# Gate sums begun one unit of four slots later, and eleven weight casts moved one quarter slot earlier, in a gated attention and feed-forward kernel

## The chip, the core and the metric

The kernel runs on one core of a Trainium2 chip. The metric is device time in microseconds (us) of one launch, the median of several runs. Engines are named as in the profile: PE (TensorE matmuls) and PEld (its weight loads), DVE (VectorE), ACT (ScalarE), POOL (GpSimd), and SP, whose queue issues most of the DMAs. A line "L230" is line 230 of the kernel before.

## The reference

```python
x = A_x                                   # 1 x 2048 x 512, float32
g = sigmoid((x * gate_w).sum(-1, keepdims=True))
# attention: 32 heads of 16, causal window of 256 keys
q, k, v = split(x @ wqkv)
o = softmax(mask(q @ k.T * 16 ** -0.5)) @ v
a = o @ wo
# feed-forward, 1792 hidden
b = (silu(x @ w_gate) * (x @ w_up)) @ w_down
return g * a + (1 - g) * b
```

Everything is float32 in and out. The row sum under the sigmoid is what the kernel calls the gate sum: one product and sum over 512 columns for each of 2048 rows, so 16 blocks of 128 rows.

## The kernel before, in words

**Precision.** A float32 matmul is done as three matmuls on halves: each operand is split into a high half (a cast to fp32r, `wh` for a weight, on ACT at L67) and a low half (operand minus high half, `wl`, on POOL at L70), and high x high, high x low and low x high are summed in PSUM. So every weight block of 128 x 512 comes in by DMA as `raw` (L75, one buffer), is cast by ACT and subtracted by POOL before PE can use it. The next `raw` can only be fetched when POOL has read the last one.

**Stages.** A first stage (to about 93 us) makes the projections of the first two groups of heads and V. The second stage, up to about 605 us, is attention, with the feed-forward's gate and up projections and the later groups' q and k projections mixed in. The third stage does the down projection and the output projection.

**Slots, quarters, units.** The attention stage is an order written out by hand: 128 slots t = 0 to 127 (8 groups of 4 heads x 16 blocks of 128 rows), each of four quarters hd = 0 to 3. In each quarter PE gets one score matmul of the next group for the row maximum (`stage1`, L280; DVE adds the mask and takes the maximum, L282), one score matmul of the present group (`stage2`, L319; ACT takes the exponential, L321, POOL masks it, L323 and L326) and six matmuls of a projection (L230). PSUM for each of the two score matmuls has two buffers, so the L319 of a quarter needs the exponential of two quarters before, and L280 needs the maximum of two quarters before. From slot 112 on there is no `stage1`. Four slots are a unit (`unit`): two pairs of projections, into the PSUM tiles `pa` in the unit's slots 0 and 2 and `pb` in its slots 1 and 3. In the first slot of each unit, after quarter 1, come the probability x V matmuls of the last unit (`av`, L343), and `finish` (L358 to L373) normalises them in five steps, the first an ACT copy, the second a DVE addition (L360) that frees `pb`.

I write (t, hd) for a quarter. Everything else is hung on quarters by `later(t, hd, f)`: what is registered for a quarter is emitted after that quarter's matmuls, in the order of registration. For a unit of feed-forward gates two tanh (L531) are emitted at its (2, 3) and (3, 0), that is in the unit's slot 2, quarter 3, and slot 3, quarter 0, and their products (L534) at (3, 0) and (3, 1).

**Weights.** For each weight block the loop over `KEYS` (L517 to L522) hangs two things on quarters: the split (ACT cast and POOL subtraction) and the DMA that fetches the next block. `t` is the slot in which the weight is first used. If the buffers come free only in the last slot before t, the split stands at (t - 1, 1) and the fetch at (t - 1, 3). Thirteen of the blocks are of this kind, first used at slots 8, 20, 32, 40, 52, 64, 72, 84, 96, 104, 112, 120 and 128.

**Gate sums.** `gate_place` (L591) fetches gate_w into a tile that the q and k halves have left free, `gate_fetch` (L595) fetches a block of x, two buffers in turn, `gate_block` (L598) multiplies and sums it on DVE (L599). Block b's fetch is hung behind the sum of block b - 2. `gate_end` (L606) turns the 16 sums into the sigmoid (an exponential on ACT, L607, and three short DVE operations, L608 to L610). Between slots 96 and 112 two blocks are summed in a unit, after that three. g7 in the code is 112.

**Row maxima.** Every eighth slot `put_max` (L293, L294) negates and transposes the maxima on DVE and sends them through DRAM (L296, L298); it is emitted at quarter 2 of a unit's first slot, just ahead of the addition L360.

Of the kernel before, what the change touches and what calls it, by code (L numbers as in the profile page):

```python
# [19 lines left out]
NB = S // P  # L20
# [13 lines left out]
def gated_mix(ctx, tc, xT, xn, wqk, wv, wo, wgu, wd, gw, out):  # L34
# [70 lines left out]
    def halves_of(t):  # L105
        n = t.shape[-1] // 2
        return [t[:, :n], t[:, n:]]
# [49 lines left out]
    PEND = []  # L157
# [21 lines left out]
    with ExitStack() as A:  # L179
# [312 lines left out]
        for n, turn in enumerate(turns):  # L492
            for m, _ in enumerate(turn, 3 * NK * n):
                at = [max(0, i - wait) * 2 * NB // (total - wait) for i in (m, m + 1)]
# [19 lines left out]
        def later(t, hd, *fs):  # L514
            AT.setdefault((t, hd), []).extend(fs)

        for n, key in enumerate(KEYS[:-1]):  # L517
            if n:
                t, free = FIRST[key], LAST.get(KEYS[n - 2], 0) + 1 if n > 1 else 0
                at = (t - 1, int(n > 1)) if t % 4 else (t - 2, 0) if free < t - 1 else (t - 1, 1)  # L520
                later(*at, lambda: PEND.pop(0)())
                later(*((t, 0) if t % 4 else (at[0], at[1] + 2)), prefetch)  # L522

        SIL = {}

# [61 lines left out]
        g7 = (G - 1) * NB  # L587
# [7 lines left out]
        def gate_fetch(b):  # L595
            nc.sync.dma_start(XG[2 + b % 2], xn[b * P:(b + 1) * P])

        def gate_block(b):  # L598
            nc.vector.scalar_tensor_tensor(XG[1], XG[2 + b % 2], 1.0, XG[0], op0=ALU.mult, op1=ALU.mult,  # L599
                                           accum_out=gate[:, b:b + 1])  # L600
# [9 lines left out]
            nc.vector.tensor_scalar(igate, gate, -1.0, 1.0, op0=ALU.mult, op1=ALU.add)  # L610

        pieces = [h for two in (QT[0], KT[0], QT[1], KT[1]) for t in two for h in halves_of(t)]
        blocks = [(t, n) for t in range(g7 - 12, g7 + NB, 4) for n in (range(1, 3) if t < g7 else range(3))][:NB]
        blocks = [(t + n, 3 - (n > 0)) for t, n in blocks]
        later(g7 - 13, 1, gate_place)
        for b in range(NB):
            t, hd = blocks[b]
            later(t, hd, lambda b=b: gate_block(b))
            if b > 1:
                t, hd = blocks[b - 2]  # L620
                later(t + hd // 3, (hd + 1) % 4, lambda b=b: gate_fetch(b))
            else:
                later(g7 - 13 + b, 2, lambda b=b: gate_fetch(b))
        later(g7 + NB - 3, 2, gate_end)
        for m in range(NB // 2):
            wd_early(m)

# [235 lines left out]
```

## Time and profile before

| | |
|---|---|
| three runs, us | 828.31, 828.32, 831.07 (median 828.32) |
| the profiled execution, us | 830.57, of which the span of instructions is 828.9 |
| PE busy, share of the span | 99% |
| PEld, DVE, ACT, POOL busy | 84%, 64%, 48%, 42% |
| mean granted TensorE clock | 0.998 |
| DMA traffic | 105.98 MB, mean 128 GB/s |

The profile gives for each instruction its start and duration in us from the span's start, its line, what it writes and reads, and, where its engine stood idle ahead of it, for how long and which other instruction or DMA ended that. Matmuls overlap, so a PE that is "busy" 99% can still lose time: what counts is the distance between the starts of matmuls. A quarter slot is measured from the first L280 or L319 of it to the first of the next.

### The profile page before, as it was taken

What the parts mean: (1) busy time and instruction counts of PE and PEld (TensorE: products, weight loads), DVE (VectorE), ACT (ScalarE), POOL (GpSimd) and SP (SyncE); (2) the same over time, 40 slices, a digit from 0 to 9 for tenths busy, and PEclk for the clock granted to TensorE, in tenths of its full rate; (3) what the DMA queues carried; (4) which work ended last, traced back from release to release, by engine and by line L of the source; (5) the groups of instructions that cost most, each with busy time, mean ns of one, the idle gap of its engine ahead of it and who ended that gap; (6) DMA issues with size and microseconds to landing.
All of it is one profiled execution on the core that took longest, in us unless ns stands there. A gap on an engine that the chain in (4) does not pass through costs nothing.

```text
span 828.9 us, 21356 instructions
## 1 busy us (share of the span) xinstructions
PE 821.0 (99%) x8329; PEld 694.9 (84%) x8329; DVE 530.7 (64%) x1494; ACT 401.0 (48%) x831; POOL 349.4 (42%) x639
## 2 busy tenths in 40 slices
PE   9999999999999999999999998999999999999998
PEld 7888998888889879888888887887888888888886
DVE  6396787778777777887787787876664332321322
ACT  6423556566556665566566554555532322222231
POOL 7712455465546564545556544465511211011020
PEclk9999999999999999999999999999999999999999
DMA  8584414514333435152453352453476331241501
GB/s 292 162 226 134 141 66 133 160 49 151 107 107 118 121 131 148 39 173 75 112 163 110 98 163 100 135 188 124 142 245 203 106 126 59 99 144 53 157 8 51
DMA packets 52980, 105.98 MB, mean 128 GB/s; under 512 B 9936, under 2 KB 14672, under 8 KB 52880
## 3 DMA queue, kind: packets, MB, share of 16 engines
q1 hardware_dynamic: 48912, 90.73, 35.8%
q0 software_dynamic: 3968, 13.90, 4.6%
q8 instruction: 65, 1.06, 0.6%
q14 instruction: 35, 0.29, 0.1%
HBM read 47.45 MB, written 31.98 MB: 96 GB/s over the span
## 4 chain that ended last, share of the span: by engine, by line
PE 96%; DMA 1%; DVE 1%; SPq 0%; POOL 0%; issue 0%; ACT 0%; DVEq 0%
PE pb L230 24%; PE pa L230 23%; PE pb L343 7%; PE ps L86 6%; PE ps L85 6%; PE ps L87 6%; PE ps L280 6%; PE ps L319 5%; PE pb L210 2%; PE ps L343 2%; PE pb L86 2%; PE pb L85 2%; PE pb L87 2%; PE pa L745 1%; PE pb L745 1%; PE pa L210 1%
## 5 line engine op out<-in xcount | busy, mean ns | idle before, releaser
L282 DVE CUSTOM_DVE_ANT_0 ps<-ps,mask 128x384 f32<-128x384 f32 (+2 forms) x512 | 269.3, 540 | 109.0 <-PE ps L280 51.3
L321 ACT ACTIVATE pt<-ps 128x384 f32<-128x384 f32 (+2 forms) x512 | 239.4, 475 | 134.9 <-PE ps L280 70.2
L323 POOL TENSOR_SCALAR_AFFINE_SELECT pt<-pt 128x256 f32<-128x256 f32 x256 | 109.4, 427 | 221.9 <-ACT pt L321 220.4
L280 PE MATMUL ps<-k,q 63*128 63x384 f32 (+2 forms) x512 | 159.7, 332 | 2.0 <-DVE mx L282 2.0
L319 PE MATMUL ps<-q,k 64*128 64x384 f32 (+2 forms) x512 | 160.5, 332 | 0.1
L230 PE MATMUL pb<-xhi,wh 64*128 64x512 f32 x512 | 115.2, 395 | 0.4 <-DVE o L360 0.4
L230 PE MATMUL pb<-xlo,wh 64*128 64x512 f32 x512 | 113.6, 391 | 0.0
L230 PE MATMUL pb<-xhi,wl 64*128 64x512 f32 x512 | 113.5, 392 | 0.0
L230 PE MATMUL pa<-xhi,wh 64*128 64x512 f32 x512 | 113.2, 395 | 0.0
L230 PE MATMUL pa<-xhi,wl 64*128 64x512 f32 x512 | 112.4, 396 | 0.0
L230 PE MATMUL pa<-xlo,wh 64*128 64x512 f32 x512 | 112.0, 393 | 0.0
L70 DVE TENSOR_TENSOR hl<-got,hh 128x512 fp32r<-128x512 f32 x51 | 44.3, 870 | 97.8 <-ACT hh L67 97.8
L280 PEld LDWEIGHTS ps<-k,q 63*128 63x128 f32 x512 | 89.0, 185 | 19.1 <-issue 5.7
L326 POOL TENSOR_SCALAR_AFFINE_SELECT pt<-pt 128x256 f32<-128x256 f32 x224 | 96.0, 429 | 0.0
L319 PEld LDWEIGHTS ps<-q,k 64*128 64x128 f32 x512 | 90.8, 185 | 4.9 <-issue 0.8
L343 PE MATMUL ps<-pt,vg 64*32 64x320 f32 (+4 forms) x1408 | 75.0, 346 | 0.0
L343 PE MATMUL pb<-pt,vg 64*32 64x320 f32 (+3 forms) x1360 | 73.9, 350 | 0.0
L282 DVE DVE_READ_ACCUMULATOR2_ANT mx<- 128x1 f32 x512 | 71.7, 140 | 0.0
L343 PEld LDWEIGHTS pb<-pt,vg 64*32 64x32 f32 x1360 | 46.3, 106 | 28.1 <-DVE ev L546 6.2
L230 PEld LDWEIGHTS pb<-xhi,wh 64*128 64x128 f32 x512 | 60.5, 185 | 6.7 <-DVE o L360 1.1
L230 PEld LDWEIGHTS pa<-xhi,wl 64*128 64x128 f32 x512 | 58.4, 185 | 8.6 <-POOL wl L70 3.0
L230 PEld LDWEIGHTS pb<-xhi,wl 64*128 64x128 f32 x512 | 60.3, 184 | 5.0
(162 smaller groups left out, 1557.0 us busy)
## 6 DMA issues: line engine op xcount, KB each, us to landing
kept_h<-ev SPq DMA_DIRECT2D x52, 256.0 KB
got<-kept_h SPq DMA_DIRECT2D x51, 256.0 KB
od<-o POOLq DMA_DIRECT2D x32, 256.0 KB, 3.6
raw<-wgu SPq DMA_DIRECT2D x28, 256.0 KB
q<-xhi SPq DMA_DIRECT2D x56, 128.0 KB
k<-xhi SPq DMA_DIRECT2D x56, 128.0 KB
vd<-vs POOLq DMA_DIRECT2D x8, 672.0 KB, 4.8
vg<-vd SPq DMA_DIRECT2D x32, 168.0 KB
```

The source lines that it names most:

```text
L70: lo_eng.tensor_tensor(out=lo, in0=src, in1=hi.bitcast(F32), op=ALU.subtract)
L85: nc.tensor.matmul(ps, lh, rh, start=start and i == 0, stop=False, skip_group_check=skip)
L86: nc.tensor.matmul(ps, lh, rl, start=False, stop=False, skip_group_check=skip)
L87: nc.tensor.matmul(ps, ll, rh, start=False, stop=stop and i == n - 1, skip_group_check=skip)
L230: mm = nc.tensor.matmul(ps[me], w[r], x[r], start=not second and i == 0, stop=bool(second) and i == n - 1)
L280: nc.tensor.matmul(ps[:, :n], QT[g % 2][pr][r, q0:q0 + P], KT[g % 2][pr][r, k0:k0 + n], start=True, stop=True)
L282: mx = nc.vector.tensor_tensor_reduce(out=ps[:, :n], in0=ps[:, :n], in1=mask[:, 3 * P - n:], scale=1.0, scalar=NEG, op0=ALU.add, op1=ALU.m ...
L319: nc.tensor.matmul(ps[:, :n], KT[g % 2][pr][r, k0:k0 + P], QT[g % 2][pr][r, k0:k0 + n], start=True, stop=True)
L321: BEHIND.append(nc.scalar.activation(pt[:, j, :n], ps[:, :n], AF.Exp, scale=SCALE))
L323: nc.gpsimd.affine_select(out=pt[:, :, :P], in_=pt[:, :, :P], pattern=[[0, 2], [1, P]], compare_op=ALU.is_ge, fill=0.0, base=0, channel_mu ...
L326: nc.gpsimd.affine_select(out=pt[:, :, 2 * P:], in_=pt[:, :, 2 * P:], pattern=[[0, 2], [-1, P]], compare_op=ALU.is_ge, fill=0.0, base=-1, ...
L343: nc.tensor.matmul(AV[g, c][h][32 * j:32 * j + 32, q0 - c * CH:q1 - c * CH], VG[4 * g + kb // 4][o, kb % 4, 17 * j:17 * j + 32], PT[g, kb, ...
```

## The change

Two edits to the tables of quarters.

The gate sums begin four slots later: `blocks` starts at g7 - 8 = 104 in place of g7 - 12 = 100, so the first two sums stand at (105, 2) and (106, 2) where (101, 2) and (102, 2) were, and two more stand at the end, at (125, 2) and (126, 2). gate_w is fetched at (101, 1) instead of (99, 1), the first two blocks of x at (102, 2) and (103, 2) instead of (99, 2) and (100, 2), and the sigmoid moves from (125, 2) to (126, 3).

Weights of the third kind (buffers free only in the last slot) are split at (t - 1, 0) instead of (t - 1, 1), and the next fetch is hung at (t - 1, 2) instead of (t - 1, 3). The split is registered from (t - 2, 3), so that it comes behind the second tanh, which is registered for (t - 1, 0) as well.

```diff
-                at = (t - 1, int(n > 1)) if t % 4 else (t - 2, 0) if free < t - 1 else (t - 1, 1)
-                later(*at, lambda: PEND.pop(0)())
-                later(*((t, 0) if t % 4 else (at[0], at[1] + 2)), prefetch)
+                def halve_next():
+                    PEND.pop(0)()
+                if t % 4:
+                    later(t - 1, int(n > 1), halve_next)
+                    later(t, 0, prefetch)
+                elif free < t - 1:
+                    later(t - 2, 0, halve_next)
+                    later(t - 2, 2, prefetch)
+                else:
+                    later(t - 2, 3, lambda t=t: later(t - 1, 0, halve_next))
+                    later(t - 1, 2, prefetch)
...
-        blocks = [(t, n) for t in range(g7 - 12, g7 + NB, 4) for n in (range(1, 3) if t < g7 else range(3))][:NB]
+        blocks = [(t, n) for t in range(g7 - 8, g7 + NB, 4) for n in (range(1, 3) if t < g7 else range(3))][:NB]
...
-        later(g7 - 13, 1, gate_place)
+        later(g7 - 11, 1, gate_place)
...
-                later(g7 - 13 + b, 2, lambda b=b: gate_fetch(b))
-        later(g7 + NB - 3, 2, gate_end)
+                later(g7 - 10 + b, 2, lambda b=b: gate_fetch(b))
+        later(g7 + NB - 2, 3, gate_end)
```

ACT, the last slot before the unit of slot 72 (quarters (70, 3) to (71, 3)); `ev` is where the tanh goes, `pt` the exponentials, one for each quarter. Before:

```order
L321 ACTIVATE pt<-ps_6347 128x384
L531 ACTIVATE ev<-pa 128x512
L321 ACTIVATE pt<-ps_6366 128x384
L531 ACTIVATE ev<-pa 128x512
L321 ACTIVATE pt<-ps_6381 128x384
L67 CAST wh<-raw 128x512
L321 ACTIVATE pt<-ps_6401 128x384
```

and now:

```order
L321 ACTIVATE pt<-ps_6347 128x384
L539 ACTIVATE ev<-pa 128x512
L321 ACTIVATE pt<-ps_6366 128x384
L539 ACTIVATE ev<-pa 128x512
L67 CAST wh<-raw 128x512
L321 ACTIVATE pt<-ps_6385 128x384
L321 ACTIVATE pt<-ps_6401 128x384
```

The cast stands one exponential earlier, and the exponential of (71, 1) behind it. Eleven of the thirteen casts move so; the two of slots 120 and 128 keep their place on ACT, since from slot 112 on the score matmuls of two quarters come together.

POOL at the same place; `pt` are the masks, two for each pair of heads. Before:

```order
L326 AFFINE_SELECT pt<-pt 128x2x128
L323 AFFINE_SELECT pt<-pt 128x2x128
L326 AFFINE_SELECT pt<-pt 128x2x128
L70 TENSOR_TENSOR wl<-raw,wh 128x512
L323 AFFINE_SELECT pt<-pt 128x2x128
```

and now:

```order
L326 AFFINE_SELECT pt<-pt 128x2x128
L70 TENSOR_TENSOR wl<-raw,wh 128x512
L323 AFFINE_SELECT pt<-pt 128x2x128
L326 AFFINE_SELECT pt<-pt 128x2x128
L323 AFFINE_SELECT pt<-pt 128x2x128
```

The subtraction that makes `wl` now stands ahead of two masks, not behind them.

SP, slots 99 to 104, where the first gate fetches (`xhi<-gw`, `xlo<-xn`) stand between stores of hidden values (`kept_h`), loads of V (`vg`) and the fetch of the next weights (`raw`). Before:

```order
L306 DMA vg<-vd 128x336
L593 DMA xhi<-gw 128x512
L596 DMA xlo<-xn 128x512 x2
L549 DMA kept_h<-ev 128x512 x2
L596 DMA xlo<-xn 128x512 x2
L306 DMA vg<-vd 128x336
L75 DMA raw<-wgu 128x512
```

and now:

```order
L306 DMA vg<-vd 128x336
L601 DMA xhi<-gw 128x512
L557 DMA kept_h<-ev 128x512 x2
L604 DMA xlo<-xn 128x512
L306 DMA vg<-vd 128x336
L75 DMA raw<-wgu 128x512
L604 DMA xlo<-xn 128x512
```

The third and fourth fetch, which wait for the sums of the first two blocks, no longer stand ahead of the load of V and the weights of slot 105.

## The prediction

> **What bounds the kernel now.** I read the page first, then the waits of PE and its weight loads, then the timelines of the places that these waits name.
>
> ```profile
> span 828.9 us, 21356 instructions
> PE 821.0 (99%) x8329; PEld 694.9 (84%) x8329; DVE 530.7 (64%) x1494; ACT 401.0 (48%) x831; POOL 349.4 (42%) x639
> ```
>
> PE is the bound: 821.0 of 828.9 us. A change can only save what PE loses between matmuls. The waits (in us: total, times, longest) say where a weight load stood idle and what ended that:
>
> ```profile
> PE ps L280 <- DVE mx L282: 2.0, 1, 2.0
> PE pb L230 <- DVE o L360: 0.4, 2, 0.2
> ...
> PEld pa L230 <- POOL wl L70: 3.0, 7, 0.4
> ```
>
> One wait of 2.0 us, two for the addition that frees `pb`, seven of 0.4 us for a weight's low half. All three kinds lie where the change works.
>
> The one long wait, on PE (start, duration; first score matmuls of the quarters (101, 3), (102, 0), (102, 1) and (103, 0)):
>
> ```profile
> 497.02 0.34 PE L280 MATMUL ps<-k,q 63*128 63x384 f32 x1
> 497.89 0.33 PE L319 MATMUL ps<-q,k 64*128 64x384 f32 x1
> ...
> 500.94 0.44 PE L280 MATMUL ps<-k,q 63*128 63x384 f32 x1 [2.00 <-DVE mx L282]
> ...
> 505.27 0.33 PE L280 MATMUL ps<-k,q 63*128 63x384 f32 x1
> ```
>
> An undisturbed quarter is 0.87 us (497.02 to 497.89). The four quarters from 497.89 to 505.27 took 7.38 instead of 3.48: 3.90 lost. Part of it is the clock, seen in the windows behind the wait (the number ahead of the last two is the granted clock):
>
> ```profile
> 498.30:501.70 3.40, 1.41 (x14) 0.86 (x10) 2.02 (x7) 0.74 (x2) 0.52 (x2) 1.00 0.39 141
> 501.70:505.10 3.40, 3.40 (x20) 2.93 (x18) 3.06 (x11) 1.22 (x3) 1.33 (x4) 0.50 0.37 139
> ```
>
> 3.40 us at half clock do 1.70 us of work, so 1.70 of the 3.90 is the clock and 2.20 the wait. Who held DVE is the first gate sum (its fetch on SP, then DVE):
>
> ```profile
> 492.75 0.97 SPq L596 DMA_DIRECT2D xlo<-xn  x2
> ```
> ```profile
> 499.65 0.69 DVE L599 SCALAR_TENSOR_TENSOR xhi<-xlo,xhi 128x512 f32<-128x512 f32 x1 [2.29 <-DMA kept_h<-ev]
> 500.26 0.56 DVE L282 CUSTOM_DVE_ANT_0 ps<-ps,mask 128x384 f32<-128x384 f32 x1
> ```
>
> DVE stood 2.29 us for a DMA. The view names a store that ended then, but L599 reads the block of x issued at 492.75, some 6.5 us before. Behind L599 stood the maximum that L280 needed.
>
> **Part 1, the gate sums.** The first two sums leave slots 101 and 102. Their fetches are issued at (102, 2) and (103, 2), their sums stand at (105, 2) and (106, 2), where the third and fourth stood:
>
> ```profile
> 519.24 0.69 DVE L599 SCALAR_TENSOR_TENSOR xhi<-xlo,xhi 128x512 f32<-128x512 f32 x1
> ```
>
> This one waited for nothing. From (102, 2) to (105, 2) there are twelve quarters of 0.87 and an `av`, so the fetch has over 10 us where the slow one took 6.5. The wait and its half clock go: **3.90 in the profiled execution** (2.20 without the clock). DVE has the same operations in units 104 to 124 as before, and two sums less in unit 100. In the last unit come two sums and the sigmoid after (126, 2):
>
> ```profile
> 602.36 0.69 DVE L534 SCALAR_TENSOR_TENSOR ev<-ev,pa 128x512 f32<-128x512 f32 x1 [1.69 <-ACT ev L531]
> ```
>
> There DVE idles 1.69 us ahead of the product of (127, 0), and a sum (0.69) and the short sigmoid steps fit in. The last fetch is issued behind the sum of (124, 3) and has six quarters, some 5 us: 0, with the rivals for the case that it is late.
>
> **Part 2, the casts: seven waits for `wl`.** One of the seven, at the unit of slot 72 (ACT, POOL, weight loads, PE):
>
> ```profile
> 370.98 0.60 ACT L531 ACTIVATE ev<-pa 128x512 f32<-128x512 f32 x1
> 371.45 0.51 ACT L321 ACTIVATE pt<-ps 128x384 f32<-128x384 f32 x1
> 371.82 0.64 ACT L67 CAST wh<-raw 128x512 fp32r<-128x512 f32 x1
> 372.33 0.52 ACT L321 ACTIVATE pt<-ps 128x384 f32<-128x384 f32 x1
> ```
> ```profile
> 372.09 0.41 POOL L323 TENSOR_SCALAR_AFFINE_SELECT pt<-pt 128x256 f32<-128x256 f32 x1 [1.27 <-ACT pt L321]
> ...
> 372.83 1.30 POOL L70 TENSOR_TENSOR wl<-raw,wh 128x512 fp32r<-128x512 f32 x1
> ```
> ```profile
> 372.29 0.18 PEld L319 LDWEIGHTS ps<-q,k 64*128 64x128 f32 x1
> ...
> 374.17 0.18 PEld L230 LDWEIGHTS pa<-xhi,wl 64*128 64x128 f32 x2 [0.42 <-POOL wl L70]
> ```
> ```profile
> 373.38 0.33 PE L319 MATMUL ps<-q,k 64*128 64x384 f32 x1
> ...
> 374.51 0.33 PE L319 MATMUL ps<-q,k 64*128 64x384 f32 x1
> ```
>
> The quarter from 373.38 took 1.13: 0.26 lost, seven times, **1.82**. With the change the cast takes the place of the exponential at 371.45 and ends at 372.09, 0.37 earlier; POOL, idle until 372.09, makes `wl` first, so it ends at about 373.4 instead of 374.13. The load wanted it at 374.17 - 0.42 = 373.75. The wait goes, with 0.35 to spare; the two masks behind it take about 0.4 each and end by 374.2, before the `av` of (72, 1).
>
> What the cast costs is the exponential behind it: it starts 0.51 later (371.82 to 372.33 is the cast's turn), at 371.96, and ends at 372.45. Two quarters on, the L319 whose weight load stood at 372.29 needs its PSUM: 0.16 late. In the `wl` wait 0.42 of lateness cost 0.26, so 0.16 of a late load was hidden; by that row this one costs about nothing, and 0.16 if nothing hides it. I take 0.05, nearer to the row: **-0.35** for the seven (0 to -1.1). The other four casts stand in slots whose exponentials are short (the last fence of this part): 0.
>
> **Part 2, the next fetch.** Where two new weights fall in one unit, the second fetch waits for POOL's read of the first, and ACT waits for that fetch. Slots 103 and 104, on ACT, POOL, SP, DVE and PE:
>
> ```profile
> 506.86 0.51 ACT L321 ACTIVATE pt<-ps 128x384 f32<-128x384 f32 x1
> ...
> 513.60 0.62 ACT L67 CAST wh<-raw 128x512 fp32r<-128x512 f32 x1 [2.79 <-DMA raw<-wgu]
> ```
> ```profile
> 508.23 1.29 POOL L70 TENSOR_TENSOR wl<-raw,wh 128x512 fp32r<-128x512 f32 x1
> ...
> 514.30 1.28 POOL L70 TENSOR_TENSOR wl<-raw,wh 128x512 fp32r<-128x512 f32 x1 [2.60 <-ACT wh L67]
> ```
> ```profile
> 509.55 0.33 SPq L75 DMA_DIRECT2D raw<-wgu  x1
> ```
> ```profile
> 378.91 0.18 DVE L293 TENSOR_SCALAR mt<-mx 128x32 fp32r<-128x32 f32 x1
> ...
> 514.32 1.30 DVE L293 TENSOR_SCALAR mt<-mx 128x32 fp32r<-128x32 f32 x1
> 515.79 0.65 DVE L360 TENSOR_TENSOR o<-pb,o 128x512 f32<-128x512 f32 x1
> ```
> ```profile
> 514.34 0.34 PE L280 MATMUL ps<-k,q 63*128 63x384 f32 x1
> ...
> 518.01 0.33 PE L280 MATMUL ps<-k,q 63*128 63x384 f32 x1
> ```
>
> The negation L293 takes 0.18, but 1.30 here, and it ends (515.62) with POOL's `wl` (515.58). So POOL held it, the addition L360 came late, and PE waited for `pb`. From 514.34 to 518.01 three quarters took 3.67 for 2.61: 1.06 lost. In the Trainium skill, "SBUF — State Buffer", section "Who interferes with whom", VectorE and GpSimd share a pair of ports as a lock: an operation of VectorE that takes both waits out a whole GpSimd instruction. The two L293 rows agree; the rule speaks against any move that puts a `wl` beside such a DVE operation, and by it 1.1 us would come back wherever they meet.
>
> With the change the first cast starts at 506.86, lasts 0.64 and ends at 507.50, and `wl` runs there instead of at 508.23: 0.73 earlier. So is the fetch, then the second `wl`: 513.57 to 514.85 if all keeps its distance. L293 then ends by 514.9, 0.7 earlier, the addition too, and of 1.06 there remains at most 0.36; I take **1.0** gained (bounds 0.7 and 1.06). The other `pb` wait, at slot 64, is of the same kind, but the exponential that the cast passes there is short:
>
> ```profile
> 338.22 0.29 ACT L321 ACTIVATE pt<-ps 128x128 f32<-128x128 f32 x1
> 338.38 0.64 ACT L67 CAST wh<-raw 128x512 fp32r<-128x512 f32 x1
> ...
> 346.36 0.34 PE L319 MATMUL ps<-q,k 64*128 64x384 f32 x1
> 347.72 0.34 PE L319 MATMUL ps<-q,k 64*128 64x384 f32 x1
> ```
>
> Its quarter took 1.36 for 0.87, 0.49 lost, and the cast moves by 0.16: **0.2** gained (0.16 to 0.49).
>
> **The sum.** 3.90 + 1.82 - 0.35 + 1.0 + 0.2 = 6.57, so the profiled execution, 830.57 with the 1.7 around its span, would come to 824.0. The median of the runs is 828.32, 2.25 lower. A run without the half clock would be 1.70 lower, which is most of that; I take it that those runs had the wait and not the half clock. Against them the gain is 6.57 - 1.70 = 4.87, to 823.45; if the 0.55 that is left is a shorter wait, 824.0. I predict **823.7**, 0.56% faster. A measurement of this kernel tells about 0.5% from no change, that is 4.14 us, 824.2.
>
> **The rivals.** (a) The wait moves from `wl` to the exponential behind the cast. For it: its slack is just used up. At the bound of 0.16 in all seven, the gain is 0.77 less: 824.2 from the median to 824.8 from the profiled execution, take 824.6. (b) The half clock is not the wait's and stays: 830.57 - 4.87 = 825.7. The rows speak against it, since the half clock begins in the window after the one in which PE stood 2 us. In the Trainium skill, "TensorE: Matmul & The Clock Gate", section "Part 1: The HAM clock gate", the clock is halved after an idle window of about 3.4 us, so a wait of 2.0 should not do it; this trace, with 2.00 idle and then 3.4 at 0.50, does not agree. The page also has the window running free of the kernel, by which one run would have the half clock and another not. (c) The gate's wait moves with it, to (105, 2) or (126, 2), because another transfer is in the way: only 1.82 - 0.35 + 1.2 = 2.67 is gained, 825.7 from the median to 827.9 from the profiled execution, take 826.5. Against it: 10 us and 5 us of room, and 519.24 without a wait. (d) Slower: eleven casts each make a new short wait of PE, and these drop the clock as the long one did. Each drop costs 1.70, so four of eleven (6.8) eat the gain and six give 824.0 + 10.2 = 834.2. Against it: seven waits of 0.4 now, and the clock was 0.998 in the mean, no more than the one stretch explains.
>
> **How the numbers follow.** Forecast 0.62, its own range 822.2 (all terms at their best, 2.20 + 1.82 + 1.06 + 0.49 = 5.57 from the median, and 0.5 of the profile's rest) to 824.2; (a) 0.13, (b) 0.10, (c) 0.11, (d) 0.04. The forecast lies beyond 0.5%, (a) to (c) within it: faster 0.62, same 0.34, slower 0.04. The range takes in (a), (b) and most of (c): 822.0 to 826.5.
>
> **What would show it.** In the profile after: no wait of L280 for a maximum above 0.5 us and no window at half clock near 500; no weight load of L230 waiting for `wl`, or at most 0.1; L293 at slot 104 below 0.7 us; no L319 waiting over 0.1 for the exponential behind a cast. I am wrong if L599 waits for a DMA anywhere, if L319's waits add up to over a microsecond, or if the half clock stands where no long wait is.

## The result, and the profile after

The changed kernel takes 823.88 us, the median of four executions (823.54 to 824.17), against 828.64 of the kernel before beside it; the ratio is 0.9936, 95% interval 0.9916 to 0.9956. The forecast was 823.7. The profiled execution took 823.76 us, with a span of 822.0 against 828.9. In the changed kernel every line behind L517 is 8 higher, up to the gate's: the gate sum L599 is L607 and the fetch of x L596 is L604.

The distances between the first score matmuls of quarters, before and after, give the account; it needs no knowledge of causes:

| quarters | before, us | after, us | difference | forecast |
|---|---|---|---|---|
| (102,0) to (102,3) | 7.38 | 3.48 | -3.90 | -3.90 |
| (8,0), (20,0), (40,0), (52,0), (72,0), (84,0), (104,0), each 1.13 to 1.29 | 8.17 | 6.09 | -2.08, and +0.20 at (7,2) | -1.82 |
| the same seven slots, quarter 1 (with `av`) | | | +0.10 to +0.15 each, +0.81 | +0.35 |
| (104,3), (105,0), (105,1) | 3.67 | 2.63 | -1.04 | -1.0 |
| (65,0) | 1.36 | 0.91 | -0.45 | -0.2 |
| all that lies ahead of the first slot | | | -0.46 | none |

These make -6.92; no other quarter differs by more than 0.08, and all the others together give back 0.08: the span is 6.84 shorter.

The page of the changed kernel, where PE is as much the bound as before:

```profile
span 822.0 us, 21355 instructions
PE 816.5 (99%) x8329; PEld 694.5 (84%) x8329; DVE 528.9 (64%) x1494; ACT 401.4 (49%) x831; POOL 349.4 (42%) x639
```

Its waits: of L280 on a maximum only this group is left (total, times, longest), where the longest was 2.4 before, and no weight load of the attention stage waits for POOL's `wl` any more.

```profile
PEld ps L280 <- DVE mx L282: 2.4, 11, 0.4
```

PE at the place of the long wait, first matmuls of (102, 0), (102, 1), (102, 2), (102, 3) and (103, 0):

```profile
497.08 0.34 PE L280 MATMUL ps<-k,q 63*128 63x384 f32 x1
...
497.95 0.33 PE L319 MATMUL ps<-q,k 64*128 64x384 f32 x1
...
498.82 0.34 PE L280 MATMUL ps<-k,q 63*128 63x384 f32 x1
...
499.69 0.33 PE L319 MATMUL ps<-q,k 64*128 64x384 f32 x1
...
500.56 0.34 PE L280 MATMUL ps<-k,q 63*128 63x384 f32 x1
```

Four quarters of 0.87, and windows there show the clock at 1.00 (the number ahead of the last two):

```profile
498.10:501.50 3.40, 3.40 (x36) 2.91 (x34) 3.13 (x10) 2.58 (x6) 2.04 (x5) 1.00 0.22 87
```

The seam that the casts moved to, at slot 72 (ACT, POOL, weight loads, PE):

```profile
369.52 0.60 ACT L539 ACTIVATE ev<-pa 128x512 f32<-128x512 f32 x1
370.00 0.63 ACT L67 CAST wh<-raw 128x512 fp32r<-128x512 f32 x1
370.50 1.54 ACT L321 ACTIVATE pt<-ps 128x384 f32<-128x384 f32 x3
```
```profile
370.71 1.29 POOL L70 TENSOR_TENSOR wl<-raw,wh 128x512 fp32r<-128x512 f32 x1 [1.34 <-ACT wh L67]
```
```profile
370.82 0.18 PEld L280 LDWEIGHTS ps<-k,q 63*128 63x128 f32 x1
371.07 0.18 PEld L319 LDWEIGHTS ps<-q,k 64*128 64x128 f32 x1
```
```profile
371.05 0.34 PE L280 MATMUL ps<-k,q 63*128 63x384 f32 x1
371.07 0.44 PE L319 MATMUL ps<-q,k 64*128 64x384 f32 x1
...
372.80 0.34 PE L280 MATMUL ps<-k,q 63*128 63x384 f32 x1
372.93 0.33 PE L319 MATMUL ps<-q,k 64*128 64x384 f32 x1
373.89 0.45 PE L343 MATMUL pb<-pt,vg 64*32 64x320 f32 x1
```

Three exponentials stand behind the cast without a gap, the weight load of L319 comes 0.25 behind that of L280, and two quarters later the two score matmuls, which use different halves of the array's rows, still start 0.13 apart. They meet in `av` (L343): its matmuls take 64 rows each, by turns of one half and the other, and the first of both halves start together, at 373.89. That is 1.09 behind the quarter's first matmul, where it was 0.95 before the change, and the rest of `av` takes the same time as before.

VectorE at slots 64 and 104:

```profile
344.12 0.68 DVE L293 TENSOR_SCALAR mt<-mx 128x32 fp32r<-128x32 f32 x1
```
```profile
508.58 0.18 DVE L293 TENSOR_SCALAR mt<-mx 128x32 fp32r<-128x32 f32 x1
```

At slot 104 the second `wl` ended at 508.29, ahead of L293; at slot 64 it ran from 343.48 to 344.76 and still held L293 up, for less time. The `raw` of slot 104's second `wl`, its fetch on SP and its cast on ACT:

```profile
503.27 0.33 SPq L75 DMA_DIRECT2D raw<-wgu  x1
```
```profile
506.31 0.62 ACT L67 CAST wh<-raw 128x512 fp32r<-128x512 f32 x1 [1.28 <-DMA raw<-wgu]
```

From the fetch to the cast are 3.04 us, where they were 4.05 before (509.55 to 513.60).

### The profile page after: what moved, and what is told of

Same layout as the page of the kernel before. It is cut to its first block, busy times and chain, and to the rows that moved or that the text cites. A ratio compares the mean times of both kernels' runs of the same rounds, so it can differ in the third digit from the quotient of the medians.

```text
span 822.0 us, 21355 instructions
## 1 busy us (share of the span) xinstructions
PE 816.5 (99%) x8329; PEld 694.5 (84%) x8329; DVE 528.9 (64%) x1494; ACT 401.4 (49%) x831; POOL 349.4 (42%) x639
## 4 chain that ended last, share of the span: by engine, by line
PE 99%; DMA 1%; SPq 0%; ACT 0%; DVE 0%; DVEq 0%; issue 0%
PE pb L230 24%; PE pa L230 24%; PE pb L343 7%; PE ps L280 6%; PE ps L85 6%; PE ps L87 6%; PE ps L86 6%; PE ps L319 5%; PE pb L210 2%; PE pa L210 2%; PE ps L343 2%; PE pb L87 2%; PE pb L85 2%; PE pb L86 2%; PE pa L753 1%; PE pb L753 1%
## 5 line engine op out<-in xcount | busy, mean ns | idle before, releaser
L319 PE MATMUL ps<-q,k 64*128 64x384 f32 (+2 forms) x512 | 160.5, 332 | 0.0
L280 PE MATMUL ps<-k,q 63*128 63x384 f32 (+2 forms) x512 | 159.1, 331 | 0.0
L280 PEld LDWEIGHTS ps<-k,q 63*128 63x128 f32 x512 | 88.7, 185 | 17.2 <-issue 5.7
L319 PEld LDWEIGHTS ps<-q,k 64*128 64x128 f32 x512 | 90.5, 184 | 4.5 <-issue 0.8
L343 PE MATMUL ps<-pt,vg 64*32 64x320 f32 (+4 forms) x1408 | 75.0, 346 | 0.0
L343 PE MATMUL pb<-pt,vg 64*32 64x320 f32 (+3 forms) x1360 | 73.9, 350 | 0.0
L343 PEld LDWEIGHTS pb<-pt,vg 64*32 64x32 f32 x1360 | 46.3, 106 | 28.2 <-DVE mx L282 5.2
```

The source lines that it names most:

```text
L280: nc.tensor.matmul(ps[:, :n], QT[g % 2][pr][r, q0:q0 + P], KT[g % 2][pr][r, k0:k0 + n], start=True, stop=True)
L319: nc.tensor.matmul(ps[:, :n], KT[g % 2][pr][r, k0:k0 + P], QT[g % 2][pr][r, k0:k0 + n], start=True, stop=True)
L343: nc.tensor.matmul(AV[g, c][h][32 * j:32 * j + 32, q0 - c * CH:q1 - c * CH], VG[4 * g + kb // 4][o, kb % 4, 17 * j:17 * j + 32], PT[g, kb, ...
```

## Experiments

Medians in us; each ratio is against the kernel before on the same chip.

| kernel | median (executions) | ratio, 95% interval |
|---|---|---|
| gate sums alone | 825.23 (4) | 0.9953 [0.9939, 0.9967] |
| casts alone | 827.98 (10) | 0.9982 [0.9969, 0.9995] |
| first two sums one slot later | 826.21 (5) | 0.9968 [0.9955, 0.9981] |
| VectorE stalled four times | 844.33 (3) | 1.0184 [1.0168, 1.0199] |
| L293 on ScalarE | 832.70 (6) | 1.0051 [1.0032, 1.0070] |
| L293 one quarter later, all places | 830.33 (10) | 1.0017 [1.0006, 1.0027] |
| the same, last place as it was | 824.72 (4) | 0.9945 [0.9926, 0.9964] |
| changed, casts behind the exponential, `wl` first | 824.24 (6) | 0.9940 [0.9927, 0.9953] |
| changed, six casts so | 824.17 (6) | 0.9938 [0.9922, 0.9954] |
| changed, six casts so, L293 later everywhere | 828.04 (11) | 0.9990 [0.9981, 0.9998] |
| changed, six casts so, L293 later but the last | **822.76** (6) | 0.9922 [0.9905, 0.9938] |
| changed, L293 later but the last | 823.15 (5) | 0.9922 [0.9908, 0.9936] |

Two more executions of the casts-alone kernel took 1003 and 2706 us, for a reason that isn't known, and are left out.

### The two halves of the change

Gate sums alone: the kernel before with the second part of the diff only.

> The kernel before with the gate sums' new places alone; every cast stays in its old place. Theory: the two changes lie in different units and add. The four quarters of slot 102, which lost 2.17, 0.28, 0.85 and 0.60 us against 0.87 each, become 0.87 each (-3.90 us against the profiled execution of before, whose second part, 1.70 us of half clock, goes only where the run of before had it). The seven quarters that wait for wl keep 0.26 to 0.42 us each, slots 64 and 104 keep their 0.5 and 1.0 us. Time 826.4 us against a before without half clock (828.6 - 2.2), down to 824.9 if every run of before had it. Rival 1 (the forecast's rival c): the sums make a wait of 1 us or more in slots 105, 106 or 126, and the gain is under 1.3 us. Rival 2: the half clock comes from something else in unit 100; then a stretch at about half clock stays in this profile.

Measured 825.23, inside the expected 824.9 to 826.4 and 3.40 under the before beside it, clocks 0.999 to 1.0 in all four executions. The quarters of slot 102 gave -2.17, -0.28, -0.85 and -0.60, which is 3.90 to the hundredth; the `wl` waits stayed. Rivals 1 and 2 fall: no new wait, no half clock. But (65, 0) gave 0.36 and (104, 3) with (105, 0) 0.42, although no cast was moved.

Casts alone: the first part of the diff only.

> The kernel before with the casts' new places alone; the gate sums stay. Theory: the seven waits for wl (2.08 us in quarters) go and the quarter with av that follows each is 0.10 to 0.15 us longer (0.8 to 1.0 back), slot 104 gives 1.04, slot 64 gives 0.46: 2.5 us in all, 826.1 us. The wait of 2 us at slot 102 stays, and with it the half clock behind it in some runs: the times fall 1.7 us apart in two groups, or the profile shows the half clock. Rival (the forecast's b): the half clock is not the wait's; then it may be gone here although the wait is there, in all six runs. Rival 2: the 0.46 us that the changed kernel gained ahead of the first attention slot belong to the casts; then they are here too, and otherwise they differ from run to run.

The median missed the expected 826.1 by 1.9. The waits for `wl` went, with 0.10 to 0.19 back in each quarter with `av`, and slot 104 gave 1.04, as in the changed kernel. The wait for the gate stayed, and the windows around it read:

```profile
496.80:500.00 3.20, 0.91 (x10) 0.43 (x6) 1.24 (x5) 0.49 (x1) 0.77 (x2) 1.00 0.30 111
500.00:503.40 3.40, 3.35 (x18) 2.81 (x20) 3.21 (x10) 0.98 (x2) 1.33 (x3) 0.52 0.27 77
```

The ten executions fall in two groups: five with a mean clock of 0.999 or 1.0, median 826.38, and five with 0.997 or 0.998, median 828.45; one of the first five, 828.18, lies in the range of the second. So the wait, 2.35 in this profile, drops the clock in about every second execution, and rival b falls. The kernel before does the same. Of the 60 executions of it beside the experiments, 25 have a clock of 0.999 or 1.0, median 828.01, and 35 less, median 829.75: 1.74 apart, where the forecast read 1.70 from one window. A mean clock of 0.998 is what 3.4 us at half clock in 829 us would give; how long the wait was in the executions without a profile isn't known.

Compared group with group, the casts alone give 1.63 (828.01 to 826.38) and 1.30 (829.75 to 828.45), and on top of the gate sums 1.35 (825.23 to 823.88). The quarters of the changed kernel promised 2.5, but part of that, at slots 64 and 104, the gate sums alone had shown without any moved cast.

The 0.46 ahead of the first slot isn't shown to be either half's: here it was 0.21, with the gate sums alone 0.41, and in the other profiles the first slot came between 0.66 earlier and 0.21 later than before.

### What the gate sum waited for

First two sums one slot later, fetches where they were:

```diff
+        blocks[:2] = [(t + 1, n) for t, n in blocks[:2]]
```

> The kernel before with one edit: the first two gate sums one slot later, at (102, 2) and (103, 2); the fetches of their blocks stay at (99, 2) and (100, 2). Theory: the first sum waited because its block came behind the stacks and stores that SP had asked for from 484 to 494 us, and it was there at 499.6; with the gate sums alone moved by four slots, the quarter (102, 2) ended at 499.8 us. So one slot is enough: no wait of L280 above 0.5 us, no half clock, the four quarters of slot 102 at 0.87 to 1.0 each, and 825.0 to 825.6 us as with all four slots. Rival 1: VectorE's own load in this unit (the normalisation of the unit before) is what the sum adds to; then L280 waits 0.3 to 0.6 us for maxima in slots 102 and 103 here and not with four slots, and the time is 826 to 827. Rival 2: the block comes even later than its place, and a wait of 1 us or more is left, 827 to 828.6.

The long wait and the half clock went (clocks 0.999 to 1.0), and the quarters of slot 102 are 0.87. But the time is 1.0 above the four-slot version, and the profile shows why in two rows of VectorE and GpSimd:

```profile
504.38 1.66 DVE L599 SCALAR_TENSOR_TENSOR xhi<-xlo,xhi 128x512 f32<-128x512 f32 x1
```
```profile
504.19 1.30 POOL L70 TENSOR_TENSOR wl<-raw,wh 128x512 fp32r<-128x512 f32 x1
```

The second sum stands beside a `wl` and takes 1.66 instead of 0.69; the maximum behind it is late, and (104, 0) takes 1.89. The time is that of rival 1, and the load is VectorE's, but the price is not the load that it named: the sum is held beside GpSimd, as L293 was. In the Trainium skill, "SBUF — State Buffer", section "Who interferes with whom", a VectorE instruction with two inputs in SBUF contends with a GpSimd instruction that reads SBUF. The gate sum is one, and its row agrees; the maxima, with one input in PSUM, are not, and the 40 of 128x384 in the kernel before that overlap a `wl` took 0.57 in the median and 0.60 at most, the other 408 the same.

L293 one quarter later, in the kernel before:

```diff
-                later(t + 1, 2, lambda g=g, i=i: put_max(g + 1, i // 8))
+                later(t + 1, 3, lambda g=g, i=i: put_max(g + 1, i // 8))
```

> The kernel before with one edit: the negation and transpose of the maxima (L293, L294) one quarter later, at the fourth quarter instead of the third of the slots 8, 16, ... 112, and so behind the addition L360 and not ahead of it. Theory: what (65, 0) and (105, 0) lost (0.49 and 0.63 us) was L293 standing behind a running wl with L360 queued behind it. With L360 ahead of it, (65, 0) becomes 0.87 to 0.95 and (105, 0) too, with no loss at the other slots, since no wl runs a quarter later than L293 there: -0.9 to -1.1 us against before, whatever L293 itself takes at slots 64 and 104. Rival: L360 and the maxima are held back by the late exponentials (the cast in front of them waits for raw); then the loss only moves to the quarter (104, 3) or to (65, 0) as before, and the gain is under 0.3.

The time rose to 830.33, by neither theory. (65, 0) and (105, 0) became 0.88 and 0.87, as expected, though (64, 2) and (64, 3) took 0.38 more. Two things were not foreseen. The wait for the gate in slot 102 vanished although no sum was moved. And a new loss of 5.5 us stood in slots 115 and 116. Both come from what SP issues when. Before, SP stood from the store of the maxima to their fetch, with the stack's transfers (the twelve of L263 and L264, which put the halves of q and k in place) behind it:

```profile
477.76 0.60 SPq L296 DMA_DIRECT2D md<-mtt  x1
479.78 1.03 SPq L298 DMA_DIRECT2D q<-md  x2
480.92 0.50 SPq L263 DMA_DIRECT2D q<-xhi  x1
...
492.01 0.64 SPq L593 DMA_DIRECT2D xhi<-gw  x1
```

So the last place was put back:

```diff
+                later(t + 1, 2 + (t < g7 - 1), lambda g=g, i=i: put_max(g + 1, i // 8))
```

> The kernel before with L293 one quarter later at all places but the last (slot 112), which stays at the third quarter; casts and gate sums stand as before the change. Two theories are tried. First: the 3.66 and 1.62 us that the run with all places moved lost in slots 115 and 116 are the last place's alone; here they are gone. Second: the gate sum's wait in slot 102 comes from SP's queue. SP stands at the transfer of the maxima for their own store to land (477.76 to 479.78 us), with the ten transfers of the stack and everything up to the gate's block behind it; one quarter later the stack is ahead of it, the gate's block is asked for at 486.95 instead of 492.75, and the quarter (102, 0) is 0.87 us although the sums were not moved. Time: 830.33 of the run with all places moved, less 3.66 + 0.23 + 1.62, is 824.8 us, with clocks of 0.999 to 1.0 in every run. Rival: the gate's wait was absent in that one profile by chance; then the times fall in two groups and the slower one is 826.5 or above.

824.72, clocks of 1.0 in all four: as expected, and the rival falls. SP now has the maxima behind the stack, and gate_w and x are asked for 7 us earlier than at 492.01 and 492.75, 6 of them counted from the place in the program:

```profile
479.47 0.60 SPq L296 DMA_DIRECT2D md<-mtt  x1
481.71 1.03 SPq L298 DMA_DIRECT2D q<-md  x2
...
484.72 0.48 SPq L593 DMA_DIRECT2D xhi<-gw  x1
485.24 1.21 SPq L596 DMA_DIRECT2D xlo<-xn  x2
```

and the first sum in its old place waits for nothing:

```profile
495.98 0.69 DVE L599 SCALAR_TENSOR_TENSOR xhi<-xlo,xhi 128x512 f32<-128x512 f32 x1
```

This one line, with neither part of the change, takes 4.4 us off its before (829.08). So the place in SP's queue, that is, how early the block is asked for, decides whether the sum waits. Why the block asked for at 492.75 was there only at 499.65 stays open.

### How long a wait drops the clock

```diff
+                for _ in range({30: 3, 46: 5, 78: 7, 94: 9}.get(t, 0) if hd == 2 else 0):
+                    nc.vector.scalar_tensor_tensor(mask, mask, 1.0, mask, op0=ALU.mult, op1=ALU.max)
```

> The changed kernel with VectorE made late on purpose in four slots: 3, 5, 7 and 9 repeats of an operation that leaves the mask as it is (128x384, about 0.48 us each) at (30, 2), (46, 2), (78, 2) and (94, 2). VectorE comes 1.4, 2.4, 3.4 and 4.3 us late; about 0.7 of that is hidden, by the old wait (2.29 idle and 0.61 of sum cost 2.20), so PE should lose 0.7, 1.7, 2.7 and 3.6 us by waiting, 8.7 in all. Theory (a wait of about 2 us drops the clock): behind the two longest there is a stretch of 3.4 us at half clock, 1.7 us more for each, and none behind the shortest; behind that of 1.7 us it is open. Sum 824 + 8.7 + 3.4 = 836 us. Rival: the half clock in unit 100 had a cause of its own there; then no stretch at half clock anywhere, and the four cost 8.7, 832.7 us. By the Trainium skill, "TensorE: Matmul & The Clock Gate", section "Part 1: The HAM clock gate" (a whole window of about 3.4 us has to be idle), only the stall of 3.6 us could do it, in some executions.

The operation took 0.60, not 0.48, so the stalls came out longer. PE idled 1.37, 2.48, 3.67 and 5.88 us. PE's rows of the two shorter ones, and the windows behind all four:

```profile
207.24 0.44 PE L280 MATMUL ps<-k,q 63*128 63x384 f32 x1 [1.37 <-DVE mx L282]
```
```profile
275.79 0.68 PE L280 MATMUL ps<-k,q 63*128 63x384 f32 x1 [2.48 <-DVE mx L282]
```
```profile
206.80:210.20 3.40, 2.96 (x27) 2.59 (x29) 3.40 (x11) 0.84 (x3) 2.04 (x3) 1.00 0.22 69
...
275.70:279.10 3.40, 3.31 (x18) 3.04 (x20) 2.79 (x9) 0.56 (x2) 0.41 (x1) 0.51 0.03 7
279.10:282.50 3.40, 3.40 (x50) 2.70 (x54) 2.39 (x8) 2.30 (x5) 2.44 (x5) 1.00 0.00 0
...
412.40:415.80 3.40, 3.29 (x19) 3.07 (x20) 2.81 (x9) 0.56 (x2) 0.41 (x1) 0.53 0.00 0
...
485.60:489.00 3.40, 3.29 (x18) 3.01 (x20) 2.81 (x9) 0.56 (x2) 0.41 (x1) 0.50 0.00 0
489.00:492.40 3.40, 3.40 (x27) 3.04 (x24) 2.22 (x7) 1.38 (x4) 0.46 (x2) 0.75 0.00 0
```

None behind 1.37; one stretch of 3.4 at half clock behind 2.48, another behind 3.67, and about one and a half behind 5.88. In quarters the four cost 1.64, 2.70 + 1.58, 3.88 + 1.50 and 6.11 + 2.18, the second terms being those of the half clock; together 19.6, of the 19.8 by which the span is longer than the changed kernel's; the medians differ by 20.4. The rival, 832.7 without any half clock, falls. With the 2.00 and 2.35 of the kernel before and the casts-alone kernel, where the clock falls in some executions (35 of 60 and 5 of 10), the point lies between 1.37 and about 2 us here. By the Trainium skill, "TensorE: Matmul & The Clock Gate", section "Part 1: The HAM clock gate", a window of about 3.4 us has to be idle; the 2.48 does not agree, and the measurement decides. The length of the stretch, and that it comes in some executions only, do fit its window.

### What the moved cast cost

In the changed kernel, the casts go back behind the exponential of (t - 1, 1), and POOL's two masks there are emitted behind `wl`:

```diff
-                    later(t - 2, 3, lambda t=t: later(t - 1, 0, halve_next))
+                    later(t - 1, 1, halve_next)
+                    FRONT.add(t - 1)
...
+                    if hd == 0 and g * NB + kb in FRONT:
+                        later(g * NB + kb, 1, masks)
+                    else:
+                        masks()
```

> The changed kernel with the seven casts back behind the exponential of the second quarter, and GpSimd's subtraction wl ahead of the two masks of that quarter in its place, which are asked for behind it. Theory (a late score product of one lane is paid for at av): with the exponential ahead of the cast, L319 of the second quarter is no longer held back, and the 0.10 to 0.15 us in the quarters (8,1), (20,1), (40,1), (52,1), (72,1), (84,1), (104,1) go: -0.8 us. wl no longer stands behind 0.73 us of masks, so that it begins with the end of the cast, 0.29 us earlier than before the change, and the seven waits for wl stay under 0.1 us each. The next transfer of raw is asked for 0.4 us later than in the changed kernel, which gives back 0.2 to 0.6 us in slots 64 and 104. Sum 823.2 to 823.9 us. Rival: the 0.10 to 0.15 us are not the exponential's; then they stay in this kernel, and the time is 824.0 to 824.6 us.

The same seam at slot 72, weight loads and PE:

```profile
370.97 0.18 PEld L280 LDWEIGHTS ps<-k,q 63*128 63x128 f32 x1
370.99 0.18 PEld L319 LDWEIGHTS ps<-q,k 64*128 64x128 f32 x1
```
```profile
372.95 0.34 PE L280 MATMUL ps<-k,q 63*128 63x384 f32 x1
372.96 0.33 PE L319 MATMUL ps<-q,k 64*128 64x384 f32 x1
```

The two lanes stay 0.01 apart, and the seven quarters with `av` are 0.08 to 0.14 shorter, 0.76 in all, and the 0.20 at (7, 2) went too, with 0.15 more at (8, 0). Two weight loads wait for `wl`, 0.3 in all, where seven waited 3.0 before the change. So the price was the exponential's, and the rival falls, though the time, 824.24, is in the range that it named: (65, 0) took 1.41 and (104, 3) 2.26, since the next `raw` is asked for 0.3 later in slot 104 and is cast 2.3 later than in the changed kernel (503.57 to 508.65, against 503.27 to 506.31). VectorE and GpSimd at slot 64:

```profile
343.76 1.18 DVE L293 TENSOR_SCALAR mt<-mx 128x32 fp32r<-128x32 f32 x1
```
```profile
343.61 1.30 POOL L70 TENSOR_TENSOR wl<-raw,wh 128x512 fp32r<-128x512 f32 x1 [2.18 <-ACT wh L67]
```

Both end at 344.9. Limited to the six casts with no second cast behind them:

```diff
-                    later(t - 1, 1, halve_next)
-                    FRONT.add(t - 1)
+                    if t % 32 in (8, 20) and t < 100:
+                        later(t - 1, 1, halve_next)
+                        FRONT.add(t - 1)
+                    else:
+                        later(t - 2, 3, lambda t=t: later(t - 1, 0, halve_next))
```

> The changed kernel with six casts behind the exponential and wl ahead of the two masks, and L293 where it was at all places. Theory: the six quarters with av at 0.10 to 0.14 less and nothing else: 823.2 us, 0.7 below the changed kernel; if the later transfers of the maxima matter for the changed kernel too, it is slower than its twin with L293 moved, by the losses of (65, 0) in some executions (up to 0.5 us). Rival: what the six quarters give comes back elsewhere, 823.9.

In the profile the attention stage is 0.88 shorter than in the changed kernel, and its span is 0.46 shorter, with 0.40 lost ahead of the first slot. The median, 824.17 (823.28 to 824.85), shows nothing of it; it is on the rival's side and I cannot say where it goes.

### L293 and the second cast

Negation on ScalarE, in the kernel before:

```diff
-            nc.vector.tensor_scalar(mt, MX[g, hf].rearrange("p h b -> p (h b)"), -1.0, None, op0=ALU.mult)
+            nc.scalar.activation(mt, MX[g, hf].rearrange("p h b -> p (h b)"), AF.Copy, scale=-1.0)
```

> The kernel before with one edit: the negation of the maxima (L293, 128x32) on ScalarE instead of VectorE. Theory: in slots 64 and 104 VectorE loses its time in L293, which took 1.3 us beside a running wl and 0.18 us elsewhere, and the row maxima behind it come late; on ScalarE it takes its usual few tenths beside wl, and the quarter (65,0), 1.36 us before, and (105,0) lose 0.4 to 0.6 us each: -0.5 to -1.1 us, and L294 (the transpose) or L282 must not become long beside wl in its place. Rival: the loss is the cast's alone, which holds the exponentials back while it waits for raw; then (65,0) and (105,0) stay as they are, or ScalarE passes the delay on, and the gain is 0. Second rival: the next VectorE instruction beside wl that is of the same kind, the transpose, takes the 1.3 us instead; then nothing moves either, but L294's rows show it.

(65, 0) and (105, 0) gave 0.45 and 0.41, so L293 beside `wl` was the loss there, though (104, 3) took 0.13 more. But the expected gain of 0.5 to 1.1 failed: the kernel is 4 us slower. ScalarE takes it in its own order, behind copies and exponentials, and VectorE waits, with L360 behind. The waits (total, times, longest):

```profile
DVE mtt L294 <- ACT mt L293: 9.4, 12, 3.0
...
PEld pb L230 <- DVE o L360: 2.4, 5, 0.6
```

Before, the last group was of two waits and 1.1. A rival had ScalarE pass the delay on, but not at this price.

### Together

The six casts and L293 later at all places:

> The changed kernel with three things together: the six casts ahead of slots 8, 20, 40, 52, 72 and 84 behind the exponential, with wl ahead of the two masks; the casts of slots 31, 63, 95 and 103, behind which another cast waits for the same buffer, where the change put them; and L293 one quarter later. Theory: six quarters at 0.10 to 0.14 less, -0.7, the wl waits stay at 0 to 0.05 each, slots 64 and 104 at 0.87 to 0.95 with nothing left of (65, 0)'s loss in any execution: 823.1 us (0.6 to 0.8 below the changed kernel). Rival: the price at av was not the exponential's in every one of these slots, or the later raw costs something: 823.9 or above.

828.04: the theory fails. The six quarters gave their 0.07 to 0.12, but slots 115 and 116 lost 5.0. ScalarE, PE and SP there:

```profile
553.34 0.60 ACT L548 ACTIVATE ev<-pa 128x512 f32<-128x512 f32 x1 [3.82 <-DMA kept_h<-ev]
```
```profile
554.37 1.06 PE L319 MATMUL ps<-q,k 64*128 64x384 f32 x2 [3.00 <-ACT pt L321]
```
```profile
546.00 0.99 SPq L298 DMA_DIRECT2D q<-md  x2
...
548.46 0.92 SPq L566 DMA_DIRECT2D kept_h<-ev  x2
```

In slot 112, where quarters come in pairs, one quarter later puts the maxima 5 us later in SP's queue (546.00; 540.98 with the last place as it was), and the store of hidden values behind them too (548.46 against 543.41). The tanh that needs that buffer stood 3.82 for it, and the exponentials and PE behind the tanh. As with the gate, the place in SP's queue decided, and the clock fell again: 0.64 and 0.86 in the two stretches of 3.4 us from 553.4. With the last place put back:

> The changed kernel with six casts behind the exponential and wl ahead of the two masks, and L293 one quarter later at all places but the last. The loss of 3.30 + 0.22 + 1.46 us of the run with all places moved goes: 828.04 - 4.98 = 823.1 us, 0.8 below the changed kernel. Rival: the last place isn't what lost it; then a wait stays at slot 115 or 116 and the time is over 826.

822.76 (822.21 to 823.06), under every execution of the changed kernel, 0.9922 of the kernel before. The page:

```profile
span 820.6 us, 21352 instructions
PE 815.3 (99%) x8329; PEld 686.3 (84%) x8329; DVE 529.0 (64%) x1494; ACT 400.9 (49%) x831; POOL 348.5 (42%) x639
```

And without the casts' order:

> The changed kernel with one more edit: L293 one quarter later at all places but the last. It parts what the best kernel so far (822.76 us) owes to the casts' order from what it owes to the maxima. Theory (each quarter counts in the time): the six quarters with av are 0.10 to 0.14 us longer again, 0.6 us in all, and (28, 1), (60, 1), (92, 1) keep the 0.1 each that the later maxima gave: 823.3 to 823.5 us. Rival: the casts' order is worth nothing in the time, as the run with that alone (824.17 beside 823.88 of the changed kernel) would have it; then 822.8.

823.15 (822.97 to 824.25): between the two, a little nearer to the theory (823.3) than to the rival (822.8). The ratios to the before beside each are equal, 0.9922, so the times don't settle it. The quarters of the two profiles say the same as before: (8, 1), (20, 1), (40, 1), (52, 1), (72, 1) and (84, 1) differ by 0.07 to 0.10, 0.56 in all; the medians differ by 0.39.

## Why the prediction was right, by its steps

**The gate wait, 3.90.** Right in size and kind, and the split into 2.20 of waiting and 1.70 of clock too: the executions of before part into two groups 1.74 apart. So was the guess that most of the gap of 2.25 to the median was an execution without half clock. What the prediction did not have is that the wait depends on when SP asks for the block, behind a round trip of the maxima and the stack: asking 6 us earlier cured it without moving a sum. (From 492.75 to 499.65 are 6.90, not 6.5.) Its test "wrong if L599 waits for a DMA anywhere" was drawn too tight: one sum waits 0.42 (547.72), nobody waits for it, and the kernel before has a wait of 0.31 of the kind.

**Seven waits for `wl`, 1.82.** Right in kind; the size was 2.08, since the prediction took the 0.26 of slot 72 for all seven, and slots 8, 20 and 104 lost 0.30 to 0.42.

**The exponential behind the cast, 0.35.** Mis-sized: 0.81 in the quarters with `av`, and with the 0.20 at (7, 2), which also went when the exponential stood ahead of the cast again, 1.01, near its bound of 1.1. The step took from the `wl` wait that 0.16 of a late load hides. There both lanes wait for the same thing; here only one lane is late, nothing in the quarters behind makes it up, and `av` collects it. Rival (a) had this term: its mechanism came almost at its bound (0.66 of its 0.77), and only other terms kept the time off its 824.6.

**Slots 104 and 64, 1.0 and 0.2.** The first right in size (1.04), the second too small (0.45). The reason for the first is only half right. The fetch was asked for 0.72 earlier, counted from the start of slot 104, as forecast (0.73), but it did not keep its length: 3.04 us from the fetch to the cast instead of 4.05, so that L293 met no `wl` at all.

The packets of the traces show when this transfer is long. In the kernel before, 135 of the transfer's 144 packets had ended by 511.85, and the last nine, a sixteenth of them, ended one by one up to 513.15; a 16 KB packet of the instruction queue (q8) ran from 510.52 to 512.02. In the six profiles in which such a packet begins 0.9 to 1.1 us behind the fetch, the cast comes 3.69 to 5.08 behind it, 1.5 to 1.7 after the packet's end; in the other eight, where it begins 2.0 to 3.2 behind, 2.81 to 3.31. At slot 64 it is the same: 3.22 to 4.34 in the ten profiles where the packet begins 0.7 to 1.0 behind the fetch, 2.58 to 3.08 in the four where it begins 1.95 to 2.72 behind. That the two share a DMA engine is inferred; no run moved such a packet by itself.

All seven profiles with the cast of slot 103 moved as in the change are on the short side, but so is one of the seven without (the first two sums one slot later), which gains 1.05 there with no cast moved. At slot 64 the moved casts are on both sides. With L293 in its old place on VectorE (65, 0) lay between 0.82 and 1.41, and with all casts unmoved at 1.01 and 1.36, so the 0.45 there is partly chance.

**Ahead of the first slot, none.** 0.46 of the profile's gain is the spread of the first stage between executions. It has the opposite sign of the error in the mis-sized term and about its size, and the two cancel in the profiled execution.

**The number.** That 823.88 lies so near 823.7 is in part luck. Against the executions of before at full clock (828.01) the gate sums alone gave 2.78, where the forecast had 2.20, and the casts on top of them 1.35, where it had 1.82 - 0.35 + 1.0 + 0.2 = 2.67. The profiled execution of before from which it was worked out, 830.57, was itself 0.82 above the median of its group.

**Rivals (b), (c) and (d)** did not come: the half clock went with the wait, there is no new wait at (105, 2) or (126, 2), and no stretch at half clock, since what the casts left behind is about 0.2 a time at most, far from 2 us.

## What to carry to other kernels

A wait for a transfer can be a place in a queue: look at what the issuing queue stood for ahead of it (here a store that had to land before its own fetch) before moving the consumer. Price a stall of PE from about 2 us on with what the clock takes behind it, here 1.7 us. Where two matmul streams share the array by rows, a late load of one can stay until matmuls that take both halves by turns, so it costs in full there. Don't take the time of a transfer as a constant that moves with its start; and an operation of VectorE that waits out GpSimd has to be placed by GpSimd's timetable.

## What the runs showed of the hardware that was not expected

- Idle stretches of PE of 2.00, 2.35 and 2.48 us were each followed by 3.4 us at half clock in the profile that shows them, one of 1.37 was not; of the 60 executions of the kernel before, 35 have the mean clock that goes with such a stretch.
- Two kinds of VectorE operation took the rest of a GpSimd subtraction beside them: L293 1.18 and 1.30 for 0.18, a gate sum 1.66 for 0.69.
- A lateness of 0.13 in one half of the array's rows was carried for two quarters, while the other half ran on.
- A 256 KB fetch took 3.2 to 5.1 us up to its cast where a 16 KB packet of the instruction queue began about 1 us behind it, and 2.6 to 3.3 where the packet began about 2 us or more behind it; at each of two places the 14 profiles part so without an exception.
